# Regrouping the score bursts of the first chunk of each layer in a two-layer attention and MLP kernel

## The chip, the cores and the metric

The kernel runs on one core of one Trainium2 chip, in one launch. The metric is device time in microseconds (us), the median of several runs. Engines are named as the profile names them: PE (TensorE matmul), PEld (its weight loads), ACT (ScalarE), DVE (VectorE), POOL (GpSimd), SP (SyncE, which issues the DMAs).

## What is computed

The reference applies, twice and with the same weights, a sliding-window attention block and an MLP block to 2048 rows of 576 values (bf16):

```
x = x + A(layernorm(x)); x = x + B(layernorm(x))        # and the same once more
A: q,k,v of 32 heads of 18; scores q k^T / sqrt(18), kept where 0 <= i - j < 256;
   softmax; p v; times wo
B: layernorm; gelu(y w1 + b1) with 4608 hidden; times w2; + b2
```

## The kernel before

**Chunks.** The 2048 rows are 16 tiles of 128 rows. Four tiles make a chunk, so that there are four chunks a layer and eight in all, numbered k = 0 to 7. Chunks 0 and 4 are the first of their layers. The stages of a chunk are: layernorm and transposition of its tiles (`ln_norm_T`), projection to q, k, v (`qkv`), scores, softmax numerator and weighted sum for 8 groups of four heads (`E0` for chunk 0, `E` for the others), normalization and output projection with residual and second layernorm (`tail`), MLP up-projection with gelu (`G_part`, in three parts), MLP down-projection (`mm2`). The stages of neighbouring chunks are woven into each other.

**Scores.** A query tile sees its own key tile (masked to a triangle), the one before it in full, and the one two before it (masked to the other triangle). In a chunk that has earlier tiles, that is 12 blocks of 128 by 128 for each head. In the first chunk of a layer there is nothing before the first tile, and 9 blocks are left: key tile 0 with queries 0, 1, 2; key 1 with 1, 2, 3; key 2 with 2, 3; key 3 with 3. `units_of` lists them as bursts of parts `(key tile, first query tile, how many, column)`. `scores` makes one burst: for each part four matmuls, one for each head of the group, in four row strips of the array (32 rows each), into two pairs of PSUM banks; then two exponentials on ACT, one for each pair of heads, from PSUM into a slot of `pT`; then masks on POOL in place. Three pairs of banks exist for this (`SC`), so that the next burst can begin when the first exponential of the one before has been made. There are six slots of `pT` (`PS`). A burst has room for 4 blocks in a bank; before, the first chunks use three bursts a group with three blocks each (384 columns of 512).

**Weighted sum.** `pv` multiplies the masked blocks of a group with v in four column strips, then DVE transposes and normalizes the result.

**Order.** No order is written out. Every step is a `Task` with a cost, a latency, what it reads and writes, and a priority; `Plan.schedule` places the tasks one by one on five engines by these costs, the earliest start first, and the priority among equals. `PL.nudge` is a table of numbers that is added to the priorities of the steps, by stage and part; it does not change what is computed, only the order. Each engine then runs its list strictly in order, with semaphores between them.

**Zero matmuls.** `keep_warm` fills planned gaps of PE longer than 0.4 us in the first 140 us with matmuls of zeros (`warm`), as many as the planned gap divided by `each` gives.

**Array shapes on PE.** Plain matmuls (q, k, v of chunks 0 and 1, down-projection) use the whole array, scores use 32-row strips, `pv` and a narrow form of the down-projection use 32-column strips, and `qkv` from chunk 2 on, `tail` and `G_part` use 64-row strips.

Of the kernel before, what the change touches and what calls it, by code (L numbers as in the profile page):

```python
# [186 lines left out]
class Plan:  # L187
# [61 lines left out]
    def keep_warm(self, a, b, bank_free, extra):  # L249
# [3 lines left out]
        each = 0.2 if a < 8.0 else 0.115  # L253
        n = int((b - a - 0.1) * 0.8 / each)
# [181 lines left out]
def build_kernel(nc, A_x, A_wqkv, A_wo, B_x, B_w1, B_b1, B_w2, B_b2, out):  # L436
# [20 lines left out]
    PVLAG = 1  # L457
# [21 lines left out]
    PL.nudge = {"": -1.63, "b": -20.47, "ea0.0": 108.12, "ea0.1": -112.05, "ea0.p0": -0.32, "ea0.p1": -13.77, "ea0.p2": -108.16,  # L479
# [63 lines left out]

    def sb(name, shape, dtype):
        return nc.alloc_sbuf_tensor(name, shape, dtype)
# [790 lines left out]
```

## Time and profile before

| | |
|---|---|
| device time, median of 3 runs | 857.62 us (857.37 to 857.83) |
| profiled execution: device time / span | 858.81 us / 857.1 us |
| PE busy | 843.6 us (98% of the span), 11968 matmuls |
| ACT busy | 600.2 us (70%), 757 instructions |
| DVE, POOL busy | 399.1 us (47%), 380.0 us (44%) |
| DMA | 119.82 MB, 140 GB/s |

The profiled execution takes 1.19 us longer than the median of the runs. PE is the engine that is almost never idle. A busy PE is not a PE at its peak, since each matmul is counted until its modelled end, beyond the start of the next one. ACT, DVE and POOL have slack over the whole, but not in every stage.

### The profile page before, as it was taken

What the parts mean: (1) busy time and instruction counts of PE and PEld (TensorE: products, weight loads), DVE (VectorE), ACT (ScalarE), POOL (GpSimd) and SP (SyncE); (2) the same over time, 40 slices, a digit from 0 to 9 for tenths busy, and PEclk for the clock granted to TensorE, in tenths of its full rate; (3) what the DMA queues carried; (4) which work ended last, traced back from release to release, by engine and by line L of the source; (5) the groups of instructions that cost most, each with busy time, mean ns of one, the idle gap of its engine ahead of it and who ended that gap; (6) DMA issues with size and microseconds to landing.
All of it is one profiled execution on the core that took longest, in us unless ns stands there. A gap on an engine that the chain in (4) does not pass through costs nothing.

```text
span 857.1 us, 27818 instructions
## 1 busy us (share of the span) xinstructions
PE 843.6 (98%) x11968; PEld 514.4 (60%) x11968; DVE 399.1 (47%) x949; ACT 600.2 (70%) x757; POOL 380.0 (44%) x567
## 2 busy tenths in 40 slices
PE   8999999999999999999999999999999999999998
PEld 6555556656566556665665655666556556556556
DVE  6686425644357442673337723564224534162012
ACT  4988887779657787366773877748777689853730
POOL 4786544476136563154432654426444276322100
PEclk9999999999999999999999999999999999999999
DMA  7899435461496523975457544675435953357320
GB/s 193 197 191 152 119 126 151 115 157 57 153 179 134 182 84 98 186 139 153 114 125 186 97 149 125 121 207 105 133 126 121 276 163 105 121 134 184 117 83 29
DMA packets 181994, 119.82 MB, mean 140 GB/s; under 512 B 107504, under 2 KB 181872, under 8 KB 181872
## 3 DMA queue, kind: packets, MB, share of 16 engines
q1 hardware_dynamic: 181872, 118.05, 55.4%
q8 instruction: 94, 1.54, 0.7%
q14 instruction: 28, 0.23, 0.1%
HBM read 90.10 MB, written 2.36 MB: 108 GB/s over the span
## 4 chain that ended last, share of the span: by engine, by line
PE 92%; DMA 2%; ACT 2%; DVE 2%; issue 1%; POOL 1%; SPq 0%; ACTq 0%; DVEq 0%; POOLq 0%
PE ps L1093 32%; PE ps L777 25%; PE ps L780 10%; PE ps L837 8%; PE ps L909 6%; PE ps L957 5%; PE ps L1048 4%; PE ps L796 1%; ACT pT L919 1%; DMA xnTa<-xn 1%; DMA wqkv<-in_A_wqkv_dram 1%; DMA xnTm<-qn 1%; DVE oq L968 1%; DMA kT<-qn 0%; DVE x_res L1025 0%
## 5 line engine op out<-in xcount | busy, mean ns | idle before, releaser
L940 POOL TENSOR_SCALAR_AFFINE_SELECT pT<-pT 128x512 bf16<-128x512 bf16 (+1 forms) x368 | 283.9, 793 | 224.4 <-ACT pT L919 218.8
L919 ACT ACTIVATE pT<-ps 128x1024 bf16<-128x1024 f32 (+1 forms) x384 | 346.2, 974 | 43.7 <-PE ps L909 42.9
L1093 PE MATMUL ps<-xnTm,w_sb 64*128 64x512 bf16 x2592 | 292.3, 376 | 0.3 <-DVE oq L968 0.2
L1103 ACT ACTIVATE hT<-ps,b1col 128x512 bf16<-128x512 f32 x276 | 167.9, 688 | 173.3 <-PE ps L1093 173.0
L1093 PEld LDWEIGHTS ps<-xnTm,w_sb 64*128 64x128 bf16 x2592 | 126.4, 94 | 141.3 <-issue 4.3
L777 PE MATMUL ps<-w_sb,hT 128*128 128x288 bf16 x1458 | 195.3, 287 | 0.0
L1025 DVE TENSOR_TENSOR x_res<-ps,x_res 128x288 f32<-128x288 f32 x224 | 100.4, 454 | 187.0 <-PE ps L777 127.2
L777 PEld LDWEIGHTS ps<-w_sb,hT 128*128 128x128 bf16 x1458 | 134.8, 98 | 51.3 <-issue 16.1
L837 PE MATMUL ps<-wqkv,xnTa 64*128 64x288 bf16 x1296 | 91.1, 283 | 2.2 <-DMA xnTa<-xn 0.8
L780 PE MATMUL ps<-w_sb,hT 128*32 128x288 bf16 x2616 | 90.3, 286 | 0.2
L861 DVE CAST qn<-ps 128x288 bf16<-128x288 f32 x112 | 46.7, 451 | 80.4 <-PE ps L837 72.6
L968 DVE STREAM_TRANSPOSE oq<-ps 128x512 f32<-128x512 f32 x64 | 45.8, 716 | 80.5 <-PE ps L957 79.5
L837 PEld LDWEIGHTS ps<-wqkv,xnTa 64*128 64x128 bf16 x1296 | 61.3, 94 | 30.0 <-issue 3.8
L780 PEld LDWEIGHTS ps<-w_sb,hT 128*32 128x32 bf16 x2616 | 66.9, 97 | 15.0 <-issue 4.4
L909 PE MATMUL ps<-qT,kT 32*128 32x384 bf16 (+2 forms) x1216 | 64.3, 276 | 2.5 <-ACT pT L919 2.5
L699 POOL TENSOR_SCALAR vtmp<-mv_all 128x1 f32<-128x1 f32 (+2 forms) x45 | 9.2, 204 | 123.4 <-DVE mv_all L690 122.1
L1109 POOL TENSOR_TENSOR x_res<-x_res,b2bc 128x576 f32<-128x576 f32 x32 | 40.2, 1277 | 35.8 <-ACT hT L1103 35.7
L686 DVE BATCH_NORM_STATS2 st_all<-x_res 128x6 f32<-128x288 f32 (+1 forms) x128 | 53.5, 445 | 2.7 <-DMA x_res<-in_A_x_dram 1.9
L849 DVE CAST vA<-ps 128x288 bf16<-128x288 f32 x60 | 25.6, 448 | 60.5 <-PE ps L837 54.6
L957 PE MATMUL ps<-pT,vA 128*20 128x384 bf16 (+2 forms) x1408 | 49.9, 275 | 0.3 <-DVE vA L849 0.2
L909 PEld LDWEIGHTS ps<-qT,kT 32*128 32x128 bf16 x1216 | 19.5, 92 | 42.8 <-issue 29.0
L1048 PE MATMUL ps<-wo_sb,attT 64*128 64x288 bf16 x576 | 43.2, 283 | 0.3
(58 smaller groups left out, 476.8 us busy)
## 6 DMA issues: line engine op xcount, KB each, us to landing
w_sb<-in_B_w_dram SPq DMA_DIRECT2D x46, 864.0 KB, 6.2
w_sb<-in_B_w_dram SPq DMA_DIRECT2D x48, 768.0 KB, 4.7
w_sb<-in_B_w_dram SPq DMA_DIRECT2D x96, 48.0 KB, 4.4
wqkv<-in_A_wqkv_dram SPq DMA_DIRECT2D x3, 576.0 KB, 5.8
x_res<-in_A_x_dram SPq DMA_DIRECT2D x3, 576.0 KB, 4.2
wqkv<-in_B_w_dram SPq DMA_DIRECT2D x2, 864.0 KB, 6.8
out_dram<-x_res SPq DMA_DIRECT2D x12, 144.0 KB, 1.9
xnTm<-xn SPq DMA_TRANSPOSE x36, 2.8
```

What stands on the lines that cost most here:

```text
L777: return e.matmul(bank(b)[:, 0:HB], lhs, rhs, start=start, stop=stop, skip_group_check=True)
L780: ins = e.matmul(bank(b)[32 * j:32 * j + 32, 0:HB], lhs[:, 32 * j:32 * j + 32], rhs, start=start, stop=stop, tile_position=(0, 32 * j), sk ...
L837: ins = e.matmul(bank(bs[o])[:, 0:HB], xnTa[r:r + 64, c, i * 128:(i + 1) * 128], wqkv[r:r + 64, c, col:col + HB], start=(c == 4), stop=(ph ...
L909: ins = e.matmul(two(bs[j // 2])[:, j % 2, col:col + nq * 128], k_of(T0 + so)[0][32 * j:32 * j + 32, g, :], qs[32 * j:32 * j + 32, g, qo * ...
L919: add("act", lambda e, h2=h2: e.activation(pT[:, sl, 2 * h2:2 * h2 + 2, lo:hi], two(bs[h2])[:, :, lo:hi], ACT.Exp, scale=SCALE), reads=[bs ...
L940: add("pool", lambda e, ap=ap, pat=pat, sgn=sgn, kind=kind: e.affine_select(ap, ap, pattern=pat, compare_op=(ALU.is_ge if kind == "d" else ...
L957: ins = e.matmul(bank(bo)[32 * j:32 * j + VW, qo * 128:(qo + nq) * 128], vA[:, (T0 + so) % VS, 8 * j + g, :], pT[:, sl, j, col:col + nq * ...
L968: add("dve", lambda e: e.transpose(oq[:, 0:4 * nt, :].rearrange("p b c -> p (b c)"), bank(bo)[:, 0:nt * 128]), reads=[bo, f"aq{(g - 1) % G ...
L1025: add("dve", lambda e: e.tensor_tensor(x_res[:, t, sl], bank(b)[:, 0:HB], x_old[:, t, sl], ALU.add), reads=[b] + ([f"xin{t}"] if first els ...
L1048: ins = e.matmul(bank(bs[o])[:, 0:HB], attT[r:r + 64, c, i * 128:(i + 1) * 128], wo_sb[r:r + 64, c, col:col + HB], start=(ph == 0 and c == ...
L1093: ins = e.matmul(bank(bks[i])[:, 0:n], w1_sb[r:r + 64, sls[i], col:col + 128], xnTm[r:r + 64, k % 2, c, 0:n], start=(c == 4), stop=(ph == ...
L1103: add("act", lambda e, ff=ff, hd=hd, bk=bk: e.activation(hd[:, 0:n], bank(bk)[:, 0:n], ACT.Gelu_apprx_tanh, bias=b1col[:, ff:ff + 1]), rea ...
```

## The change

There are four edits.

1. In chunks 0 and 4 (`SHARE`) a group has two bursts of four blocks each, which fill the banks: (key 0 with queries 0, 1, 2 and key 1 with query 1), then (key 1 with queries 2, 3 and key 2 with 2, 3). The ninth block, key 3 with query 3, is taken out; `scores9` makes it for four groups at once, in a burst of its own with 4 blocks in a bank and one mask over all of it. `pv` of each group reads its quarter of that slot, and the slot comes free after the fourth group.
2. `keep_warm` reckons 0.215 us for a zero matmul before 8 us, and fills 96% of the planned gap there.
3. The planner's latencies of the first loads (x and the query weights) are raised. The same loads are issued in the same order.
4. The whole table of nudges is replaced, and with it the order of all later steps on all engines.

```
+        each, part = (0.215, 0.96) if a < 8.0 else (0.115, 0.8)
+        n = int((b - a - 0.1) * part / each)
...
-    PL.nudge = {"": -1.63, "b": -20.47, "ea0.0": 108.12, "ea0.1": -112.05, "ea0.p0": -0.32, "ea0.p1": -13.77, "ea0.p2": -108.16,
+    PL.nudge = {"b": 299.87, "ea0.0": 223.17, "ea0.1": 300, "ea0.2": 299.99, "ea0.n0": 300, "ea0.p0": -270.55, "ea0.p1": 39.66,
...
-            cost=0.45 if a < 4 else 0.6, lat=1.4 if a < 4 else 2.0, prio=prio)
+            cost=0.45 if a < 4 else 0.6, prio=prio, **({"lat": 1.2, "move": cnt * 0.64} if a < 4 else {}))
...
+        if k in SHARE:
+            us = [[(0, 0, 3, 0), (1, 1, 1, 384)], [(1, 2, 2, 0), (2, 2, 2, 256)]]
...
+    ninth = {}
+    def scores9(k, g, prio):
+        gs = range(g, g + 4)
+        kept, PL.part = PL.part, f".n{g}"
+        parts = [(3, 3, 1, 128 * n) for n in range(4)]
+        sl = scores(k, g, parts, prio, gs)
+        PL.part = kept
+        for n in gs:
+            ninth[k, n] = ([parts[n - g]], sl)
+    SHARE = (0, 4)
...
     def pv(k, g, units, bo, first, last, prio):
         slots.extend(sl for _, sl in units)
+        if k in SHARE and last:
+            units = units + [ninth[k, g]]
+            if g % 4 == 3:
+                slots.append(ninth[k, g][1])
```

Counted over the whole program, the score bursts go from 192 to 180, the exponentials on ACT from 384 (288 of 1024 elements a partition and 96 of 768) to 360 (all of 1024, the same elements in all), the score matmuls from 1216 to 1280 and those of the weighted sum from 1408 to 1472 (the same columns in more pieces), the zero matmuls from 24 to 36. On PE's list, the places at which the array shape changes from one matmul to the next go from 406 to 388: from 71 to 63 up to the first matmul of `G_part`, from 335 to 325 behind it.

PE's list at the start of the program, before (`warm` are zeros, `ident,xn` are transpositions of a normalized tile, `wqkv,xnTa` the projections of chunk 0, `ident,qn` transpositions of k):

```order
L664 MATMUL ps<-warm 128x256 x8
L673 MATMUL ps<-warm 128x256 x11
L734 MATMUL ps<-ident,xn 128x128 x5
L673 MATMUL ps<-warm 128x256 x3
L796 MATMUL ps<-wqkv,xnTa 128x288 x10
L734 MATMUL ps<-ident,xn 128x128 x4
L796 MATMUL ps<-wqkv,xnTa 128x288 x10
L734 MATMUL ps<-ident,xn 128x128 x6
L796 MATMUL ps<-wqkv,xnTa 128x288 x10
L874 MATMUL ps<-ident,qn 128x128 x8
```

The same place on PE now:

```order
L661 MATMUL ps<-warm 128x256 x8
L670 MATMUL ps<-warm 128x256 x12
L731 MATMUL ps<-ident,xn 128x128 x5
L670 MATMUL ps<-warm 128x256 x6
L731 MATMUL ps<-ident,xn 128x128 x4
L793 MATMUL ps<-wqkv,xnTa 128x288 x5
L731 MATMUL ps<-ident,xn 128x128
L793 MATMUL ps<-wqkv,xnTa 128x288 x5
L731 MATMUL ps<-ident,xn 128x128 x4
L793 MATMUL ps<-wqkv,xnTa 128x288 x20
L871 MATMUL ps<-ident,qn 128x128 x8
L731 MATMUL ps<-ident,xn 128x128 x6
```

One more zero matmul stands ahead of the first transposition and three more behind it; the second tile's transposition comes ahead of the first projection instead of behind its ten matmuls; and between the transpositions of the third and fourth tile and the next projection there is no other matmul.

PE's list around the first score bursts (`qT,kT`), before:

```order
L796 MATMUL ps<-wqkv,xnTa 128x288 x20
L874 MATMUL ps<-ident,qn 128x128 x8
L796 MATMUL ps<-wqkv,xnTa 128x288 x5
L874 MATMUL ps<-ident,qn 128x128 x8
L909 MATMUL ps<-qT,kT 128x384 x4
L796 MATMUL ps<-wqkv,xnTa 128x288 x15
L909 MATMUL ps<-qT,kT 128x384 x4
```

And now (the row `128x128 x16` is the first of the shared bursts):

```order
L793 MATMUL ps<-wqkv,xnTa 128x288 x45
L871 MATMUL ps<-ident,qn 128x128 x8
L793 MATMUL ps<-wqkv,xnTa 128x288 x10
L922 MATMUL ps<-qT,kT 128x384 x4
L922 MATMUL ps<-qT,kT 128x128 x4
L871 MATMUL ps<-ident,qn 128x128 x8
L793 MATMUL ps<-wqkv,xnTa 128x288 x15
L922 MATMUL ps<-qT,kT 128x128 x16
```

From the start of the program, 85 matmuls of projections stand ahead of the first score burst instead of 70, and 36 transpositions instead of 44.

ACT's list around the first exponentials (`pT<-ps`; `kT<-ps` are copies of transposed k, `qn<-ps` of q or k), before:

```order
L878 COPY kT<-ps 128x8x128 x2
L919 ACTIVATE pT<-ps 128x2x384
L858 CAST qn<-ps 128x2x8x18
L919 ACTIVATE pT<-ps 128x2x384 x3
L858 CAST qn<-ps 128x2x8x18
L919 ACTIVATE pT<-ps 128x2x384 x2
L878 COPY kT<-ps 128x8x128
L919 ACTIVATE pT<-ps 128x2x384 x42
```

And now:

```order
L875 COPY kT<-ps 128x8x128
L855 CAST qn<-ps 128x2x8x18
L932 ACTIVATE pT<-ps 128x1024
L875 COPY kT<-ps 128x8x128
L932 ACTIVATE pT<-ps 128x1024
L855 CAST qn<-ps 128x2x8x18
L932 ACTIVATE pT<-ps 128x1024 x2
L875 COPY kT<-ps 128x8x128
L932 ACTIVATE pT<-ps 128x1024 x34
```

Two of the four copies of k now stand behind the first exponential, where one did; of the casts one instead of two. The last row holds 32 exponentials of chunk 0 and two of chunk 1.

More of the change, by code (lines that the diff above doesn't have):

```diff
@@ L631, in xin_load @@
             writes=[f"xin{t}" for t in range(a, a + cnt)], cls="x", ring=4,
-            cost=0.45 if a < 4 else 0.6, lat=1.4 if a < 4 else 2.0, prio=prio)
-    for a, cnt in ((0, 1), (1, 1), (2, 2)):
-        xin_load(a, cnt)
+            cost=0.45 if a < 4 else 0.6, prio=prio, **({"lat": 1.2, "move": cnt * 0.64} if a < 4 else {}))
     def w_load(n, reads=()):
@@ L639, in w_load @@
         dma("sp", wqkv[:, 0:4, n * D:(n + 1) * D], A_wqkv[0:512, n * D:(n + 1) * D].rearrange("(c p) d -> p c d", p=P), reads=reads,
-            writes=[f"w{w}A"], cost=0.5, lat=1.9, prio=-10)
+            writes=[f"w{w}A"], cost=0.5, lat=1.9, prio=-10, **({"move": 2.56} if n == 0 else {}))
         for b in range(2):
@@ L643, in w_load @@
             dma("sp", wqkv[64 * b:64 * b + 64, 4, cols], A_wqkv[512:576, cols], reads=reads, writes=[f"w{w}B{b}"], cost=0.6, prio=-10)
-    w_load(0)
-    w_load(1)
-    w_load(2)
+    for a, cnt in ((0, 1), (1, 1), (2, 2)):
+        xin_load(a, cnt)
+    for n in range(3):
+        w_load(n)
     add("pool", lambda e: e.memset(nhalf[:, :], -0.5), writes=["nhalf"], cost=0.1, prio=-10)
@@ L892, in units_of, with scores @@
             us = [[(0, 0, 3, 0)], [(1, 1, 3, 128)], [(2, 2, 2, 256), (3, 3, 1, 128)]]
+        if k in SHARE:
+            us = [[(0, 0, 3, 0), (1, 1, 1, 384)], [(1, 2, 2, 0), (2, 2, 2, 256)]]
         us = [[p for p in u if t0 + p[0] >= 0] for u in us]
         return [u for u in us if u]
+    ninth = {}
[8 more added lines that the diff above has]
+    SHARE = (0, 4)
     slots = deque(range(PS))
-    def scores(k, g, parts, prio):
+    def scores(k, g, parts, prio, gs=None):
         l, t0, nt = CH[k]
@@ L906, in fn @@
             ins = None
-            for (so, qo, nq, col) in parts:
+            for n, (so, qo, nq, col) in enumerate(parts):
+                gg = gs[n] if gs else g
                 for j in range(4):
-                    ins = e.matmul(two(bs[j // 2])[:, j % 2, col:col + nq * 128], k_of(T0 + so)[0][32 * j:32 * j + 32, g, :],
-                                   qs[32 * j:32 * j + 32, g, qo * 128:(qo + nq) * 128], start=True, stop=True, tile_position=(32 * j, 0),
+                    ins = e.matmul(two(bs[j // 2])[:, j % 2, col:col + nq * 128], k_of(T0 + so)[0][32 * j:32 * j + 32, gg, :],
+                                   qs[32 * j:32 * j + 32, gg, qo * 128:(qo + nq) * 128], start=True, stop=True, tile_position=(32 * j, 0),
                                    skip_group_check=True)
@@ L991, in E0 @@
             lead[g] = [(us[0], scores(0, g, us[0], prio))]
+            if 0 in SHARE and g % 4 == 0:
+                scores9(0, g, prio)
         for g in gs:
@@ L1006, in E @@
                 PL.part = f".{g}"
+                if k in SHARE and n == 0 and g % 4 == 0:
+                    scores9(k, g, prio)
                 units.append((parts, scores(k, g, parts, prio)))
-                while pend and pend[0][0] <= 3 * g + n - PVLAG:
+                while pend and pend[0][0] <= len(us) * g + n - PVLAG:
                     pv(k, *pend.pop(0)[1:], prio - 0.1)
@@ L1011, in E @@
                     done = n == len(us) - 1
-                    pend.append((3 * g + n, g, units, bo, not any(x[1] == g for x in pend) and units[0][0] is us[0], done))
+                    pend.append((len(us) * g + n, g, units, bo, not any(x[1] == g for x in pend) and units[0][0] is us[0], done))
                     units = []
```

2 lines of the change are left out of this document (removed), and 124 rows, old and new, of the table add.

## The prediction

> **What bounds the kernel now.** I read the page first, then PE by stretches of 20 us, then the start and the first chunk's scores row by row.
>
> ```profile
> PE 843.6 (98%) x11968; PEld 514.4 (60%) x11968; DVE 399.1 (47%) x949; ACT 600.2 (70%) x757; POOL 380.0 (44%) x567
> PE 92%; DMA 2%; ACT 2%; DVE 2%; issue 1%; POOL 1%; SPq 0%; ACTq 0%; DVEq 0%; POOLq 0%
> ```
>
> The second row is the chain of work that ended last: PE carries 92% of it. The stretches (PE, PEld, DVE, ACT, POOL busy, then clock, DMA share, GB/s) show where PE is not the bound:
>
> ```profile
> 0.00:20.00 20.00, 16.16 (x127) 12.12 (x128) 13.02 (x41) 8.05 (x17) 8.34 (x26) 0.91 0.74 198
> 20.00:40.00 20.00, 18.70 (x266) 11.37 (x264) 13.26 (x37) 19.11 (x28) 13.76 (x23) 1.00 0.85 202
> 40.00:60.00 20.00, 18.45 (x292) 10.59 (x292) 17.10 (x39) 19.53 (x27) 17.91 (x28) 1.00 0.97 169
> 60.00:80.00 20.00, 19.21 (x314) 11.28 (x310) 15.58 (x41) 15.44 (x23) 12.87 (x26) 1.00 1.04 185
> 80.00:100.00 20.00, 19.10 (x270) 10.09 (x274) 8.54 (x23) 16.80 (x26) 13.01 (x18) 1.00 0.57 121
> ...
> 580.00:600.00 20.00, 19.15 (x291) 11.71 (x290) 9.28 (x20) 16.48 (x17) 14.21 (x20) 1.00 0.38 100
> ...
> 720.00:740.00 20.00, 19.48 (x272) 10.78 (x264) 5.54 (x10) 17.27 (x23) 9.21 (x12) 1.00 0.43 136
> ...
> 840.00:860.00 20.00, 14.26 (x117) 11.15 (x114) 4.63 (x11) 0.00 (x0) 0.00 (x0) 0.97 0.06 23
> ```
>
> PE idles 13.5 us of the span. 8.4 of them lie in the first 100 us, 2.8 at the very end (14.26 busy of 17.1), and 2.2 between, where no stretch has more than 0.85. From 20 to 60 us ACT is full (19.1 and 19.5 of 20): there the exponentials of chunk 0 set the pace and PE waits for them. So whatever the change saves on PE counts in full behind the first up-projection (86 us); ahead of it, the start and ACT decide.
>
> **The change part by part.** *Shape changes on PE.* Two rows of one down-projection with a score burst between them, from PE's timeline, and two lengths of the same matmuls from the chain:
>
> ```profile
> 103.01 1.65 PE L777 MATMUL ps<-w_sb,hT 128*128 128x288 bf16 x12
> 104.59 0.40 PE L909 MATMUL ps<-x_res,kT 32*128 32x256 bf16 x8
> 104.92 1.64 PE L777 MATMUL ps<-w_sb,hT 128*128 128x288 bf16 x12
> ```
> ```profile
> 161.31 3.05 PE ps L777 x24
> 164.69 1.58 PE ps L777 x12
> ```
>
> Twelve more matmuls take 3.05 - 1.58 = 1.47 us, 0.1225 each. From 103.01 to 104.92 are 1.91 us; less 1.47 leaves 0.44 for the burst. Its 512 columns, four heads side by side, stream in 0.22 at the same rate. The other 0.22 are its two shape changes, 0.11 each. Behind the first up-projection the list has 10 changes fewer: -1.1 us, on the path. The 8 that go ahead of it are worth 0.9, but in a stretch that ACT sets; I count them at nothing.
>
> *More and smaller pieces.* 64 score matmuls and 64 of the weighted sum are added, at equal columns.
>
> ```profile
> 102.68 0.34 PE L909 MATMUL ps<-x_res,xnTm 32*128 32x384 bf16 x4
> 102.85 0.22 PE L909 MATMUL ps<-x_res,kT 32*128 32x128 bf16 x4
> ```
>
> Four matmuls of 128 columns take 103.01 - 102.85 = 0.16, and 0.05 without the shape change: they run side by side at the streaming rate, so that smaller pieces cost nothing. One page of the Trainium skill speaks against this edit: TensorEngine Tiling (Array Packing), Instruction Overhead, gives each matmul some 60 cycles of overhead and warns against small pieces; 128 matmuls by 25 ns would be an estimated 3.2 us, and the sum +2.1 instead of -1.1. The rows show no such overhead at 128 columns; what no row has is four sets of 128 in one burst.
>
> *The clock at the start.* The first projection waits for the query weights; then its ten matmuls run at half clock (PE busy, clock, DMA, GB/s in three windows of 3.41 us):
>
> ```profile
> 0.99:4.41 3.42, 3.37 (x16) 1.00 0.69 182
> 4.41:7.82 3.41, 1.34 (x13) 1.00 1.03 343
> 7.82:11.23 3.41, 2.68 (x14) 0.50 0.98 301
> ```
> ```profile
> 3.30 5.11 DMA wqkv<-in_A_wqkv_dram
> 8.55 2.56 PE ps L796 x10
> 11.45 1.23 PE ps L796 x10
> 14.30 0.45 PE ps L874 x8
> ```
>
> A window with 1.34 us of matmuls was followed by one at half clock, one with 2.68 by full clock. The loss is 2.56 - 1.23 = 1.3 us. Now one more zero matmul ahead of the first transposition, three more behind it (256 columns each, 0.11 by the streaming rate), and the second tile's four transpositions fall into the middle window, about 0.7 us more, some 2.0 in all. That lies between 1.34 and 2.68, so I give half a chance that the clock stays. By the Trainium skill (TensorE: Matmul & The Clock Gate, What's actually happening) the clock drops only after an idle window; by that it would stay for certain. The trace disagrees: the window ahead of the drop held 13 matmuls.
>
> *The first score burst.* These are the rows of PE (with the first up-projection) and ACT there:
>
> ```profile
> 20.75 0.34 PE L909 MATMUL ps<-qT,kT 32*128 32x384 bf16 x4
> ...
> 86.14 11.83 PE L1093 MATMUL ps<-xnTm,w_sb 64*128 64x512 bf16 x108
> ```
> ```profile
> 13.65 0.71 ACT L737 COPY xnTa<-ps 128x640 bf16<-128x640 bf16 x1
> 14.79 1.01 ACT L878 COPY kT<-ps 128x1024 bf16<-128x1024 bf16 x1 [0.28 <-PE ps L874]
> 21.77 0.82 ACT L919 ACTIVATE pT<-ps 128x768 bf16<-128x768 f32 x1
> 26.53 1.08 ACT L878 COPY kT<-ps 128x1024 bf16<-128x1024 bf16 x1
> 27.43 4.55 ACT L919 ACTIVATE pT<-ps 128x768 bf16<-128x768 f32 x6
> 48.91 12.26 ACT L919 ACTIVATE pT<-ps 128x768 bf16<-128x768 f32 x16 [0.15 <-PE ps L909]
> 75.33 1.01 ACT L919 ACTIVATE pT<-ps 128x1024 bf16<-128x1024 f32 x1
> 77.29 1.94 ACT L919 ACTIVATE pT<-ps 128x1024 bf16<-128x1024 f32 x2
> ```
>
> From 8.55 PE now has 85 projections at 0.1225 and 27 transpositions at 0.056 (0.45 for 8) to the first burst: 10.4 + 1.5, so 20.5. New waits come on top: the third tile's projection now stands right behind the transpositions, with only the ACT copy (0.71) and two hand-overs between them, 0.8; the fourth tile's copy then comes behind a copy of k (1.01 + 0.71 against 1.23 us of projections), 0.5; and 0.3 for the key weights and the last copy of k. First burst at 22.1 instead of 20.75, first exponential at 22.6 instead of 21.77 (it no longer stands behind three copies of k). With the half clock: 23.6.
>
> *Exponentials of chunk 0.* Before, they last from 21.77 to 59.2 (48.91 + 12.26, less the two of chunk 1 in that row, 1.94): 37.5 us, with one copy of k (27.43 - 26.53 = 0.9) and two casts (0.3 each), so that 36.0 remain for 48, 0.75 each with 1.0 us of gaps. Now 36 of 1024 elements at 1.94 - 1.01 = 0.93 make 33.5, with the same gaps 34.5: -1.5. The bounds: nothing, if time went by elements alone; -2.7 by the means of the forms below (48 by 0.824 against 36 by 1.024). Two copies of k and one cast fall among them: +0.9 - 0.3 = +0.6. So chunk 0's exponentials end at 22.6 + 34.5 + 2.1 = 59.2 with full clock, where they end now, and at 60.2 with half clock. Behind that point PE has the same work left as before. The start and ACT together: 0 (to +1.0; and -1.2 from the lower bound of the exponentials).
>
> ```profile
> L919 ACT ACTIVATE pT<-ps 128x1024 bf16<-128x1024 f32 x288 | 274.8, 1024 | 28.8 <-PE ps L909 28.6
> L940 POOL TENSOR_SCALAR_AFFINE_SELECT pT<-pT 128x512 bf16<-128x512 bf16 x256 | 163.6, 653 | 194.1 <-ACT pT L919 192.7
> L940 POOL TENSOR_SCALAR_AFFINE_SELECT pT<-pT 128x1024 bf16<-128x1024 bf16 x112 | 124.5, 1111 | 30.3 <-ACT pT L919 26.1 <-PE ps L777 2.0 <-PE ps L909 1.1
> L919 ACT ACTIVATE pT<-ps 128x768 bf16<-128x768 f32 x96 | 71.5, 824 | 14.9 <-PE ps L909 14.3
> ```
>
> *Masks.* A group had 4 masks of 512 and one of 1024: 3.72 us. Now 5 of 512 and a quarter of one of 2048, which no row shows; by 0.458 for each further 512 elements it takes 2.0: 3.77. POOL stays under ACT (4.5 exponentials by 0.93, 4.2 a group). But the first weighted sum now waits for the shared mask and all of the group's, about 0.9 us of ACT idle, in place of the 1.0 of gaps already counted. *Later shared bursts, slots of pT, order of DMAs*: one slot of six is held for four groups, which leaves 5 for two bursts a group instead of 6 for three; the fourth q transposition is issued ahead of the tiles' transpositions on SP, which land long before chunk 1's projections need them. Nothing for both. *Eight new zero matmuls at 58 to 86 us* go where PE is planned idle; 60 to 100 us has 1.7 us of idle to cover their 0.9. I take 0; uncovered they cost 0.9.
>
> The sum is -1.1: span 857.1 to 856.0, own time 858.81 to 857.7, and in the runs' median, which lies 1.19 below the profiled execution, 857.62 to 856.5.
>
> **The rivals.** *B, the new order takes more:* the same loads are planned later and closer to what they take, and if the list fits the real times better, the single waits behind 100 us shrink too (0.85 at 580, 0.52 at 720, 2.2 in all), and the gain on ACT comes as -2.7 instead of -1.5: -1.1 - 1.2 - 1.1 (half of the later idle) = -3.4, 854.2. For it: ACT was full where chunk 0 was late. Against it: the waits behind 100 us are already few, and a new order can make others. *C, the start is late and stays late:* half clock (+1.0), zero matmuls uncovered (+0.9), and the new list puts one or two new waits of the size of the worst now (0.85) behind the first up-projection, +1.1 on average: -1.1 + 3.0 = +1.9, 859.5. It decides from a first exponential later than 23.6 us. For it: 15 more projections stand ahead of the first burst, the two new waits, and PE stands in front of the first weighted sum until POOL is done. Against it: PE has all of chunk 1's projections to fill in. *D, small pieces do not run side by side* where four sets of 128 follow each other, as the page's rule would have it: each of the 32 added sets takes 4 by 0.056 instead of 0.05, 0.17 more, 5.4 us: 861.9. The rows of 128 columns speak against it.
>
> **How the numbers follow.** A measurement of this kernel can tell 0.2% from no change, 1.7 us. The forecast A has 0.50, with its own range from 855.3 (exponentials at their bound) to 857.5 (half clock): 0.12 of it is faster by over 1.7 us, 0.38 within. B has 0.30, all faster. C has 0.17 and D 0.03, both slower. So faster 0.42, same 0.38, slower 0.20. The range reaches into B beyond its middle and to C's middle, 853.4 to 859.4, and leaves out D, the far half of C and the far end of B.
>
> **What would show it.** The ten first projections in 1.23 us, or 2.56 again; the first exponential at 22.6 us; chunk 0's exponentials in 36.6 us with 0.93 each; the first up-projection at 86.1, give or take 1; behind it, PE's time from there to the end shorter by 1.1; the four sets of 128 in a shared burst in 0.2 to 0.3 us. The prediction is wrong if the first up-projection moves by over 2 us, or if the part behind it changes by other than 0.5 to 1.7.

## The result and the profile after

The changed kernel takes 862.55 us (860.42 to 863.76, six runs), the kernel before on the same chip 857.73 us (857.32 to 858.76, six runs): ratio 1.0052, 95% interval 1.0038 to 1.0065. It is slower by about 4.5 us (3.3 to 5.6 by the interval), and lies 3.15 us above the range. Its profiled execution took 861.57 us, with a span of 859.8. That is below its median, while the profiled execution of the kernel before lies above its own, so that the two profiles, which the following readings rest on, differ by 2.7 us only.

The page's row of engines and its chain of waits, of the changed kernel:

```profile
PE 844.9 (98%) x12360; PEld 523.3 (61%) x12360; DVE 396.9 (46%) x949; ACT 597.6 (70%) x733; POOL 380.9 (44%) x571
PE 89%; DMA 4%; DVE 2%; ACT 2%; POOL 1%; issue 1%; SPq 1%; POOLq 0%; DVEq 0%
```

PE's share of the chain fell from 92% to 89%, and DMA's rose from 2% to 4%. The first five stretches of 20 us (PE, PEld, DVE, ACT, POOL busy, then clock, DMA share, GB/s):

```profile
0.00:20.00 20.00, 18.02 (x142) 13.34 (x143) 14.49 (x45) 8.40 (x17) 9.06 (x27) 1.00 0.90 212
20.00:40.00 20.00, 17.23 (x198) 10.30 (x200) 11.27 (x32) 16.53 (x20) 13.50 (x22) 0.85 0.65 177
40.00:60.00 20.00, 19.32 (x398) 11.62 (x390) 17.02 (x38) 19.04 (x21) 16.04 (x25) 0.98 0.90 163
60.00:80.00 20.00, 18.53 (x311) 10.75 (x310) 16.31 (x43) 16.58 (x23) 14.60 (x27) 1.00 0.83 182
80.00:100.00 20.00, 17.65 (x218) 10.01 (x218) 8.82 (x24) 14.90 (x23) 12.30 (x20) 1.00 0.55 115
```

The start is better than before: the clock is 1.00 over the first 20 us, where it was 0.91. From 20 to 40 us PE and ACT both lose (ACT 16.53 instead of 19.11), and the clock is 0.85. Of the 844.9 us of PE, some are matmuls at half clock.

The part behind the first up-projection, once for the kernel before and once for the changed kernel, and the row with which it begins there:

```profile
86.14:857.10 770.96, 765.89 (x10888) 465.65 (x10884) 337.33 (x788) 532.20 (x656) 322.83 (x460) 1.00 0.53 135
```
```profile
89.88:859.80 769.92, 764.25 (x11200) 472.57 (x11200) 332.35 (x784) 527.28 (x642) 320.19 (x458) 1.00 0.54 135
```
```profile
89.88 2.33 PE L1114 MATMUL ps<-xnTm,w_sb 64*128 64x512 bf16 x20 [1.62 <-DMA xnTm<-xn]
```

So that part is shorter by 1.04 us, as forecast (1.1). The whole loss, 89.88 - 86.14 = 3.74 us, comes ahead of it, in a stretch that was forecast at nothing. The sizes of single profiles scatter: in the profiles of the experiments below this part takes 769.7 to 771.3 us with the kernel before's grouping (e3, e4, e16) and 768.6 to 770.0 with the changed one (e1, e2, e5, e6, e9, e10, e12 to e15).

**Where PE stands.** PE's timeline of the changed kernel around the first weighted sum (start, duration, and in brackets the wait ahead and what ended it), two rows of the kernel before, and three windows of the changed kernel's clock:

```profile
30.36 1.40 PE L774 MATMUL ps<-wqkv,xnTm 128*128 128x288 bf16 x10
31.80 0.40 PE L922 MATMUL ps<-qT,kT 32*128 32x256 bf16 x8
34.68 0.21 PE L1210 MATMUL ps<-ident,hT 36*128 36x36 bf16 x1 [2.48 <-DMA hT<-in_B_b_dram]
34.82 1.14 PE L974 MATMUL ps<-pT,vA 128*20 128x384 bf16 x20
...
36.44 2.58 PE L774 MATMUL ps<-wqkv,xnTm 128*128 128x288 bf16 x10
```
```profile
31.80 0.67 PE L957 MATMUL ps<-pT,vA 128*20 128x384 bf16 x16
...
35.54 0.19 PE L1189 MATMUL ps<-ident,hT 36*128 36x36 bf16 x1
```
```profile
30.61:34.02 3.41, 1.54 (x18) 0.81 (x15) 2.25 (x8) 3.41 (x5) 3.32 (x6) 1.00 0.78 253
34.02:37.43 3.41, 2.75 (x34) 1.41 (x35) 2.75 (x10) 1.35 (x2) 2.98 (x6) 0.50 0.27 55
37.43:40.85 3.42, 3.42 (x43) 1.78 (x45) 1.44 (x4) 2.30 (x4) 1.23 (x2) 0.50 0.52 99
```

PE stands idle from 32.2 to 34.7 us ahead of the transposition of the up-projection's bias (b1, the row `ident,hT`), which the new order places right in front of the first weighted sum. The bias itself is not later: by the completion counts in the trace it lands at 34.63 us, and at 35.20 in the kernel before. But there PE comes to it at 35.54 us, behind the first weighted sum and 15 projections, and does not wait. The clock of the changed kernel is then halved for two windows, 6.8 us: ten projections take 2.58 us instead of 1.40. Later PE stands 0.89 us ahead of 60.94 (first scores of chunk 1), 0.33 ahead of 77.75, and 1.62 ahead of the first up-projection.

The bias is not the only thing that PE would wait for here. The first weighted sum needs POOL's masks, and eight of them run in a row until 33.95 us:

```profile
29.06 4.89 POOL L953 TENSOR_SCALAR_AFFINE_SELECT pT<-pT 128x512 bf16<-128x512 bf16 x8 [0.74 <-ACT pT L932]
```

The projections next on PE's list wait for VectorE. Its timeline, first of the changed kernel, then of the kernel before:

```profile
30.14 0.46 DVE L858 CAST qn<-ps 128x288 bf16<-128x288 f32 x1 [0.16 <-PE ps L774]
31.77 1.18 DVE L683 BATCH_NORM_STATS2 st_all<-x_res 128x6 f32<-128x288 bf16 x3 [1.18 <-DMA x_res<-in_A_x_dram]
...
34.56 0.41 DVE L683 BATCH_NORM_STATS2 st_all<-x_res 128x6 f32<-128x288 bf16 x1
34.88 0.44 DVE L858 CAST qn<-ps 128x288 bf16<-128x288 f32 x1
```
```profile
31.80 0.46 DVE L861 CAST qn<-ps 128x288 bf16<-128x288 f32 x1 [0.15 <-PE ps L780]
32.18 0.45 DVE L686 BATCH_NORM_STATS2 st_all<-x_res 128x6 f32<-128x288 bf16 x1
32.55 0.70 DVE L968 STREAM_TRANSPOSE oq<-ps 128x512 f32<-128x512 f32 x1
33.17 0.42 DVE L686 BATCH_NORM_STATS2 st_all<-x_res 128x6 f32<-128x288 bf16 x1
33.51 0.23 DVE L971 RECIPROCAL rinv<-oq 128x16 f32<-128x16 f32 x1
33.66 0.39 DVE L861 CAST qn<-ps 128x288 bf16<-128x288 f32 x1
```

Before, the statistics of chunk 2's rows (`st_all`) stand almost all singly between other steps. Now eight of them follow one another with only their own aggregations between them, wait 1.18 us for the rows, and end at 35 us. Two casts of chunk 1's projections stand behind them, and hold the two PSUM banks that PE's next projections need (e1 below shows PE's wait for them).

The third place is SyncE's queue, of the changed kernel, with PE's row that waits for it:

```profile
39.63 5.52 SPq L623 DMA_DIRECT2D wo_sb<-in_A_wo_dram  x9
46.01 2.43 SPq L623 DMA_DIRECT2D w_sb<-in_B_w_dram  x3
48.48 1.52 SPq L623 DMA_DIRECT2D wo_sb<-in_A_wo_dram  x3
50.05 1.24 SPq L877 DMA_TRANSPOSE x_res<-qn  x1
...
57.33 1.32 SPq L877 DMA_TRANSPOSE x_res<-qn  x1
```
```profile
60.94 0.34 PE L922 MATMUL ps<-x_res,xnTm 32*128 32x384 bf16 x4 [0.89 <-ACT pT L932]
```

The twelve loads of the output projection's weights read the first group's attention output as a starting signal, which now comes at 38.7 us instead of 34.4. They and a load of w1 hold the queue to 50 us, and the transpositions of chunk 1's queries and keys, with some of chunk 2's tiles, follow one after another until 61. By the completion counts in the trace the one issued at 57.33 landed at 60.73, 0.2 us ahead of the burst; the exponential that the row names had ended at 60.24.

### The profile page after: what moved, and what is told of

Same layout as the page of the kernel before. It is cut to its first block, busy times and chain, and to the rows that moved or that the text cites. A ratio compares the mean times of both kernels' runs of the same rounds, so it can differ in the third digit from the quotient of the medians.

```text
span 859.8 us, 28551 instructions
## 1 busy us (share of the span) xinstructions
PE 844.9 (98%) x12360; PEld 523.3 (61%) x12360; DVE 396.9 (46%) x949; ACT 597.6 (70%) x733; POOL 380.9 (44%) x571
## 4 chain that ended last, share of the span: by engine, by line
PE 89%; DMA 4%; DVE 2%; ACT 2%; POOL 1%; issue 1%; SPq 1%; POOLq 0%; DVEq 0%
PE ps L1114 31%; PE ps L774 23%; PE ps L777 11%; PE ps L834 9%; PE ps L922 6%; PE ps L974 5%; PE ps L1069 3%; DMA xnTm<-xn 3%; ACT pT L932 1%; PE ps L793 1%; DMA hT<-in_B_b_dram 1%; SPq L623 1%; DVE xn L714 0%; POOL rstd L698 0%; POOL pT L953 0%
## 5 line engine op out<-in xcount | busy, mean ns | idle before, releaser
L932 ACT ACTIVATE pT<-ps 128x1024 bf16<-128x1024 f32 x360 | 343.0, 1029 | 41.9 <-PE ps L922 41.5
L1114 PEld LDWEIGHTS ps<-xnTm,w_sb 64*128 64x128 bf16 x2592 | 130.9, 94 | 139.9 <-issue 5.4
L774 PE MATMUL ps<-w_sb,hT 128*128 128x288 bf16 x1374 | 184.3, 287 | 1.5 <-DVE x_res L1046 1.1
L774 PEld LDWEIGHTS ps<-w_sb,hT 128*128 128x128 bf16 x1374 | 126.9, 98 | 50.5 <-issue 17.8
L777 PE MATMUL ps<-w_sb,hT 128*32 128x288 bf16 x2952 | 100.0, 286 | 0.2
L777 PEld LDWEIGHTS ps<-w_sb,hT 128*32 128x32 bf16 x2952 | 76.6, 97 | 15.0 <-issue 3.6
L922 PE MATMUL ps<-qT,kT 32*128 32x128 bf16 (+2 forms) x1280 | 62.4, 271 | 0.9 <-ACT pT L932 0.6
L974 PE MATMUL ps<-pT,vA 128*20 128x256 bf16 (+2 forms) x1472 | 51.4, 274 | 0.2 <-POOL xn L722 0.2
L714 DVE TENSOR_SCALAR xn<-x_res,mv_all,rstd 128x576 bf16<-128x576 f32 (+1 forms) x60 | 34.0, 572 | 19.9 <-POOL rstd L698 11.0
```

Of the source, the lines that this page charges most:

```text
L774: return e.matmul(bank(b)[:, 0:HB], lhs, rhs, start=start, stop=stop, skip_group_check=True)
L777: ins = e.matmul(bank(b)[32 * j:32 * j + 32, 0:HB], lhs[:, 32 * j:32 * j + 32], rhs, start=start, stop=stop, tile_position=(0, 32 * j), sk ...
L922: ins = e.matmul(two(bs[j // 2])[:, j % 2, col:col + nq * 128], k_of(T0 + so)[0][32 * j:32 * j + 32, gg, :], qs[32 * j:32 * j + 32, gg, qo ...
L932: add("act", lambda e, h2=h2: e.activation(pT[:, sl, 2 * h2:2 * h2 + 2, lo:hi], two(bs[h2])[:, :, lo:hi], ACT.Exp, scale=SCALE), reads=[bs ...
L974: ins = e.matmul(bank(bo)[32 * j:32 * j + VW, qo * 128:(qo + nq) * 128], vA[:, (T0 + so) % VS, 8 * j + g, :], pT[:, sl, j, col:col + nq * ...
L1114: ins = e.matmul(bank(bks[i])[:, 0:n], w1_sb[r:r + 64, sls[i], col:col + 128], xnTm[r:r + 64, k % 2, c, 0:n], start=(c == 4), stop=(ph == ...
```

## The experiments

Each run is timed beside the kernel before on its chip; ratios are to that, with a 95% interval. e1, e2, e5, e6, e9, e10 and e12 to e15 start from the changed kernel, e3, e4, e11 and e16 from the kernel before, e7 and e8 from a mixture. Unless shown otherwise, an edit moves steps in the list that `Plan.schedule` has made (`order`), so that nothing else changes.

**The bias loaded first, and the stand filled with zeros.**

```
e1: +  b1 = order.pop(position of the load of b1)
    +  order.insert(position of the first load of w1, b1)
e2: +  24 zero matmuls ahead of the transposition of b1
```

> The changed kernel, with one thing moved: the load of the bias b1 is issued on SP ahead of the first load of MLP weights instead of behind the second; all other lists are as they were. Theory 1 (the late bias): PE stood 2.6 us at the transposition of b1, because its load was queued behind two weight loads, and the window with that wait brought half clock from 34.0 to 40.9 us. Without it both go, and the first up-projection comes 3.5 to 5 us earlier than at 89.9: about 858. Theory 2 (the masks): the weighted sum of group 0, next on the list, would have waited for POOL's masks until 34.0 anyway. Then the wait only shrinks by 0.8 us, the clock still halves, and the time stays at 861 to 862.

> The changed kernel, with 24 zero matmuls (2.6 us at full clock) ahead of the transposition of b1, so that PE is busy while it waits, and nothing moved. If the half clock behind the wait is a loss of its own, its 6.8 us at half rate go and with them 2 to 3 us: 859.5 to 860.5. If ACT sets the pace there, the half clock was hidden, and the time stays at 862.5. If the wait is not there in an execution, the zeros cost up to 2.6 us: 863 to 865.

Measured: e1 1.0055 [1.0036, 1.0073], e2 1.0055 [1.0042, 1.0069]. Neither gains. PE's timeline of e1:

```profile
32.27 0.40 PE L925 MATMUL ps<-qT,kT 32*128 32x256 bf16 x8
34.19 0.17 PE L1213 MATMUL ps<-ident,hT 36*128 36x36 bf16 x1 [1.52 <-ACT pT L935]
...
36.65 0.66 PE L777 MATMUL ps<-wqkv,xnTm 128*128 128x288 bf16 x2 [1.18 <-DVE qn L861]
```

With the bias there, the transposition waits for an exponential to free its bank, and the projection behind it for VectorE's cast. The bias was only the last of several. The masks are another, as the second theory had it: in e1 POOL's eight masks end at 34.42 us and the first weighted sum starts at 34.47. In e2 the clock stayed whole at 34 us, and the loss moved: the first scores of chunk 1 waited 2.88 us until 61.58, and a half clock from 60.8 to 67.6 followed.

**The kernel before, with a late bias or a better start.**

```
e3: the second load of w1 issued ahead of b1, in the kernel before
e4: -        n = int((b - a - 0.1) * 0.8 / each)
    +        n = 20 if 4.0 < a < 8.0 else int((b - a - 0.1) * 0.8 / each)
```

> The kernel before, with the second load of MLP weights issued ahead of the load of b1, as the changed kernel has it. The bias then lands 2.5 to 3.5 us later than at 35.2 us, where PE comes to its transposition at 35.5. Theory 1 (a late bias alone costs this much, whatever the grouping): PE waits 2 to 3 us, the clock halves behind it, 860 to 863. Theory 2 (it is the masks and the grouping): PE has slack to ACT here, the wait is absorbed, 857.5 to 858.5.

> The kernel before, with 20 zero matmuls instead of 3 behind the first transposition, so that PE is busy until the query weights land and the clock does not halve behind that wait. As predicted for the start: the ten first projections in 1.2 instead of 2.6 us, the first score burst 1.3 us earlier, and at most that much of the whole: 856.4 to 857.4. If the start is bound by loads and transpositions, nothing: 857.7.

Measured: e3 1.0035 [1.0022, 1.0047]; e4 0.9985 [0.9973, 0.9997]. PE's timeline of e3:

```profile
37.18 0.19 PE L1193 MATMUL ps<-ident,hT 36*128 36x36 bf16 x1 [1.84 <-DMA hT<-in_B_b_dram]
37.30 0.67 PE L961 MATMUL ps<-pT,vA 128*20 128x384 bf16 x16
37.90 0.34 PE L913 MATMUL ps<-qT,kT 32*128 32x384 bf16 x4
38.17 1.38 PE L781 MATMUL ps<-wqkv,xnTm 128*128 128x288 bf16 x5
```

A stand of 1.84 us at this place costs the kernel before some 3 us, with nothing regrouped: the five projections behind it run at half clock (1.38), and its first up-projection moves to 89.60 (another wait in this execution, 1.34 us ahead of 68.02, is part of that). So the place is as dear as the changed kernel suggests. In e4's profile the first score burst comes 1.06 us earlier and the first up-projection 0.42 later (86.56): PE waits 1.00 us ahead of 64.03 and 0.17 ahead of 64.99 for two transpositions that stand behind a load of w2. In this execution, 858.70 us, the earlier start is eaten ahead of 86 us; over eleven runs (median 858.06) it is worth 0.15%.

**The queue.**

```
e5: the 12 loads of wo without reads=["aq0"], ahead of chunk 1's first transposition;
    the third load of w1 behind four more transpositions
e6: e5 with the zeros of e2
```

> The changed kernel with one edit of the SyncE queue: the twelve loads of the output projection's weights no longer wait for the first group's attention output and are issued at about 30 us, where the queue stands idle for 5 us, and the third load of up-projection weights is issued behind four more transpositions. In the changed kernel those fifteen loads hold the queue from 39.6 to 50.0 us while the queries and keys of chunk 1 that were cast from 43 us on wait behind them. Theory 1 (the late first weighted sum costs through this queue): the transpositions go out from about 45 us, the first score burst of chunk 1 no longer waits 0.96 us, the up-projection starts 1 to 1.5 us earlier than in the changed kernel (89.9 us), and the time is about 861, ratio to the kernel before 1.0035. The wait of 2.5 us at 32 to 34.7 us and the half clock behind it stay. Rival (the queue is no limit, the exponentials are): no change, ratio 1.0052, and the wait at 59 to 61 us stays.

> The edit of the queue and 24 zero matmuls ahead of the transposition of b1, which fill the wait at 32 to 34.7 us. The zero matmuls alone moved the loss: the clock stayed whole at 34 us, but the first score burst of chunk 1 then waited 2.96 us at 58 to 61.6 us and the clock halved there (ratio 1.0055). Theory 1: with the transpositions out earlier that wait shrinks to under 1 us, no half clock follows, and the up-projection starts at about 87 us, 2.5 to 3 us earlier than in the changed kernel; time about 858.8, ratio 1.001. Rival (exponentials): the wait at 58 us stays over 2 us with the half clock behind it, ratio about 1.005.

Measured: e5 1.0069 [1.0056, 1.0081] and e6 1.0092 [1.0078, 1.0105]. e6 is worse than the changed kernel, and e5's interval overlaps with that kernel's. My edit was badly made: the weight loads from 29.4 us on follow right behind b1, which landed later (PE stood 3.48 us until 35.17; that they are the reason is not shown), and the load of w1 now stood at 55.0, ahead of the very transposition that the burst waits for (issued 56.86, landed 61.71). The rival does not follow either, since the wait moved with that landing.

**Second layer alone.** The kernel before with `SHARE = (4,)` and the new table's numbers for chunks 4 to 7.

> The kernel before with the regrouping in the second layer's first chunk alone (chunk 4) and the changed table's entries for chunks 4 to 7; the start, the first chunk and the order of everything up to the second layer are those of the kernel before. Behind the first up-projection it has 12 fewer changes of array shape than the kernel before (the changed kernel has 10 fewer). If each is worth 0.1 us on the path, the first up-projection stands at 86.1 us as before and the time is 1.1 to 1.3 us lower: 856.6, ratio 0.9986. Rival (what the part behind gained in the changed kernel came from its later start, not from the regrouping): no difference, ratio 1.0000.

> The same with 20 zero matmuls instead of 3 behind the first transpositions, which keep the clock whole at the start (alone they gave a ratio of 0.9985 [0.9973, 0.9997]). If the two gains add up: 855.3 to 856, ratio 0.9972. If the start's gain is given back by 65 us, as the profile of it alone showed (first up-projection at 86.6 us), it is that of the run before: 0.9986.

Measured: e7 1.0629 [1.0608, 1.0650] and e8 1.0636 [1.0621, 1.0650], 53 to 55 us slower, with waits of 4.2 to 6.9 us on PE at about 400, 515 and 736 us and half clock behind them. Half of one table and half of the other make an order that fits neither, so that this says nothing on the regrouping: that the 1.04 us behind the first up-projection come from the shape changes stays argued, not shown. The new order of that part is a rival that no run takes out.

**The order of chunk 1's tiles.** The changed kernel transposes the queries of tiles 0, 3, 1, 2 in this order (the kernel before 2, 1, 0, 3); the first burst reads 0, 1 and 2.

```
e9:  queue: qx1, kx1, qx2, xa0, qx3, k5, k4      (was qx3, k5, xa0, qx1, kx1, qx2, k4)
e10: e9 with the zeros of e2
e11: kernel before, qx0 and kx0 behind qx3
```

> The changed kernel with six transpositions of the SyncE queue in another order. Its table transposes the queries of chunk 1 in the order tile 0, 3, 1, 2, and the kernel before in the order 2, 1, 0, 3; the first score burst of chunk 1 reads the queries of tiles 0, 1 and 2. Here the order is 0, 1, 2, 3. In the changed kernel the transposition of tile 2's queries is issued at 57.33 us, lands at 60.73, and the burst starts at 60.94. Theory 1 (the order of the queue makes the burst wait): issue at about 53, landing by 57, no wait of 0.96 us ahead of the burst; the up-projection starts about 1 us earlier, time about 861.5, ratio 1.004; the wait at 32 to 34.7 us and the half clock behind it stay. Rival (exponentials set the pace here): nothing changes, 1.0052.

> The same order of the queue and 24 zero matmuls ahead of the transposition of b1. The zero matmuls alone kept the clock whole at 34 us and then lost 2.96 us in the wait for the first score burst of chunk 1 and 2.13 us in a half clock behind it, since tile 2's queries landed at 61.38. Theory 1: those queries land by 57, that wait and the half clock go, the first up-projection stands at 86 to 87.5 us, and the time is about 858.7: ratio 1.000 to 1.001. Rival: the burst goes on waiting over 2 us, now for something else, and the ratio stays at about 1.005.

> The kernel before with the opposite edit: the transpositions of tile 0's queries and keys of chunk 1, which its first score burst reads, are issued behind those of tile 3's queries instead of ahead of them. Theory 1: they land at about 60 to 61 us instead of by 57.3, the burst waits about 2 us at 58.7, with or without a half clock behind it, and the time is 2 to 4 us longer: ratio 1.002 to 1.005. Rival: no difference, 1.000.

Measured: e9 1.0046 [1.0029, 1.0062], e10 1.0048 [1.0033, 1.0064]. As forecast, the first scores of chunk 1 waited no longer (they start at 58.91 in e9 and nothing halves there); but the time hardly moved. PE and SyncE's queue in e9:

```profile
74.00 2.00 PE L1074 MATMUL ps<-wo_sb,attT 64*128 64x288 bf16 x26
79.23 1.38 PE L839 MATMUL ps<-wqkv,xnTa 64*128 64x288 bf16 x10 [3.23 <-DMA xnTa<-xn]
```
```profile
71.66 0.66 SPq L628 DMA_DIRECT2D w_sb<-in_B_w_dram  x1
72.42 1.22 SPq L742 DMA_TRANSPOSE xnTa<-xn  x1
```

The next wait, 0.33 us in the changed kernel, grew to 3.23: PE came to it 1.4 us earlier, and chunk 2's last tile, which stands behind a load of w2 of 864 KB, landed at 79.19, 6.8 us after its issue. In the changed kernel it stands behind the same load and landed 5.4 us after its issue, so that the load is not the whole of it. e11 (1.0113) is no test: the moved transpositions read buffers that the next tile's casts have overwritten, and its stand of 7 us is on another cast.

**Work into the first stand.** All earlier cures had failed, so these two put useful work there and then mended the queue as well.

```
e12: e1, and
     DVE: three casts of chunk 1's projections ahead of chunk 2's statistics
     PE:  ten matmuls of chunk 1's projections ahead of the transposition of b1
e13: e12 and e9, and the second load of w2 behind chunk 2's last transposition
```

> The changed kernel with useful work in its first long wait. On VectorE the casts of chunk 1's first projections (tile 0) stand ahead of the statistics of chunk 2's rows, which wait for a load until 33 us, instead of behind them; on TensorE two projections of chunk 1 (ten matmuls) that followed the first weighted sum stand ahead of the transposition of b1, and b1 is loaded first. Theory (that wait is the cause): TensorE stands under 0.7 us between 32 and 35 us instead of 2.6, the clock stays whole there, the first up-projection comes 1.5 to 3 us earlier than 89.9, and the time is 859 to 861: ratio 1.001 to 1.003. Rival (each wait that goes is replaced by the next, because the exponentials and transpositions that follow set the pace): first up-projection still behind 89 us, ratio 1.005.

> The same with the queries of chunk 1 transposed in the order tile 0, 1, 2, 3, and the second load of down-projection weights issued behind the transposition of chunk 2's last normalized tile instead of ahead of it (in the run with the queue's order alone, that tile was issued at 72.4 us behind this load, landed at 79.2, and TensorE waited 4.2 us for it, with a half clock behind it). Theory: no wait over 1 us between 30 and 86 us, the clock whole from 6 us on, the first up-projection at 86 us or earlier; with the 1.1 us that the part behind it gained: 856.5 to 858, ratio 0.998 to 0.9995, no worse than the kernel before. Rival: ratio 1.003 or more, with a new wait over 1.5 us in the profile.

Measured: e12 1.0023 [1.0010, 1.0035], e13 1.0011 [1.0000, 1.0022]. PE's timeline of e12:

```profile
32.61 1.40 PE L793 MATMUL ps<-wqkv,xnTm 128*128 128x288 bf16 x10
34.20 0.17 PE L1229 MATMUL ps<-ident,hT 36*128 36x36 bf16 x1 [0.19 <-ACT pT L951]
34.48 0.67 PE L993 MATMUL ps<-pT,vA 128*20 128x384 bf16 x20
35.09 0.40 PE L941 MATMUL ps<-qT,kT 32*128 32x256 bf16 x8
38.04 0.40 PE L941 MATMUL ps<-qT,kT 32*128 32x384 bf16 x8 [2.56 <-DVE b1col L1231]
```

The stand ahead of b1 is gone, and with it more than half of the loss (0.52% to 0.23%); with the queue's orders four fifths of it (0.11%), with the first up-projection at 87.70. The step from e12 to e13 lies within their intervals. What is left in both is one stand of 2.56 us at 35 to 38 us, for the bank that the cast of b1 frees, behind the same statistics, and a half clock for one window behind it (39.2 to 42.6 us in e13). e13 keeps the regrouping, so the order of the steps between 30 and 80 us, not the regrouping itself, accounts for most of the loss; that was the theory. (What the same moves would give the kernel before was not tried.) What stays in every such version is the later first weighted sum: in e13 POOL's masks end at 34.10 us and it starts at 34.16, where the kernel before starts it at 31.80. The forecast of e13 was still too good by 0.2%, since the stand at 35 us remained.

**The statistics later still.**

```
e14: e13, chunk 2's statistics in two halves behind the first group's weighted sum
e15: the same without the queue's two edits
```

> The run with all orders mended, and on VectorE the statistics of chunk 2's rows (3.2 us) behind the first group's weighted sum and the cast of b1 instead of ahead of them, in two halves, with the two steps on GpSimd that follow each. Theory (VectorE's order is the cause): the wait of 2.75 us at 35 to 38 us falls under 0.7, the clock is whole from 6 us on, the first up-projection comes at 85 to 86 us, and the time is 856 to 857.5: ratio 0.997 to 0.9988, below the kernel before. Rival (exponentials and masks set the pace ahead of the second weighted sum, whatever VectorE does): the wait stays over 1.5 us, ratio 1.001.

> The same without the two edits of the SyncE queue (tile order of chunk 1's transpositions, second load of down-projection weights). Theory: no wait between 30 and 40 us; the waits at 59 and 74 us that hang on the queue stay or grow, since TensorE comes to them earlier, and the first up-projection comes 1.5 to 2.5 us later than in the run with both: ratio 0.9995 to 1.0015. Rival (the queue's orders are only an echo of the first wait): the same time as the run with both.

Measured: e14 1.0033 [1.0022, 1.0044], e15 1.0036 [1.0023, 1.0049]. My theory fell here, and e15 came out as its rival had it: the same time without the queue's two edits as with them. So no pair of runs shows a gain from the queue. PE's timeline of e14:

```profile
36.69 0.40 PE L958 MATMUL ps<-qT,kT 32*128 32x384 bf16 x8 [1.13 <-ACT pT L968]
...
38.92 1.39 PE L813 MATMUL ps<-wqkv,xnTm 128*32 128x288 bf16 x20 [1.23 <-DVE qn L894]
...
47.16 0.67 PE L1010 MATMUL ps<-pT,vA 128*20 128x384 bf16 x20 [0.91 <-POOL pT L989]
```

One stand became three, for exponentials, a cast and a mask, and the half clock stayed for one window (38.8 to 42.3 us). The kernel before spreads the eight statistics almost one by one; two halves are not that. Whether such a spread would bring the last 0.11% back was not tried, nor was the kernel before's place of b1 on PE's list.

**A version below both.** The kernel before with the zeros of e4 and its first load of w2 behind the two transpositions that PE waited for in e4.

> The kernel before with 20 zero matmuls instead of 3 at the start (alone: ratio 0.9985 [0.9973, 0.9997]) and its first load of down-projection weights issued behind the transpositions of chunk 2's second tile and chunk 1's last keys instead of ahead of them. With the zeros alone these were issued at 57.3 and 60.1 us behind that load (55.2 us, landed at 60.9) and landed at 64.0 and 64.9, and TensorE stood 1.66 us between 61.5 and 65 us. If the load in front of them is what makes them late: they land 2 to 3 us earlier, that wait falls to under 0.5 us, the first up-projection stands at 85.3 us instead of 86.6, and the time is about 856.5: ratio 0.997 to 0.9975. Rival (they wait for VectorE or for each other, not for the load): 0.9985 again.

Measured: 857.15 us (856.21 to 858.58, eleven runs), the kernel before 858.44 (857.52 to 861.05, fifteen runs): 0.9984 [0.9975, 0.9993], 0.16% faster than the kernel before and so faster than both. In its profile the wait is gone (the transpositions landed at 59.67 and 61.55 instead of 64.0 and 64.9, the first up-projection starts at 84.79, and the execution took 856.22). But the ratio is that of e4: that the queue's edit adds to the zeros is seen in one profile and not in the medians.

## Why the prediction was wrong

*Right in size, with the cause open: the part behind the first up-projection*, 1.04 us shorter against 1.1. Two profiles of one grouping can differ by as much: e16, which has the kernel before's grouping and PE's list of that part, takes 769.7 us there against 771.0. *Right: the exponentials and the mask.*

```profile
21.25 1.03 ACT L932 ACTIVATE pT<-ps 128x1024 bf16<-128x1024 f32 x1 [0.29 <-PE ps L922]
36.55 1.94 ACT L932 ACTIVATE pT<-ps 128x1024 bf16<-128x1024 f32 x2 [2.06 <-PE ps L922]
53.72 7.44 ACT L932 ACTIVATE pT<-ps 128x1024 bf16<-128x1024 f32 x8 [0.26 <-PE ps L922]
```

Eight take 7.44 us, 0.93 each. The shared mask took 2.01 us. *Right: small pieces.* The shared burst starts at 23.63 and the projection behind it at 23.96, 0.33 us with its two shape changes: as long as any other burst of 512 columns, so that rival D is out.

*Right in sign, too small: the start.* I put the middle window at some 2.0 us of matmuls and gave the clock half a chance; it stayed. In this execution the clock's windows, counted back from 34.02 in steps of 3.41, begin at 3.29 and 6.71 us and hold 3.22 and 2.79 us. In e1, e5, e13, e14 and e15, which start the same way, a window begins at 4.2 to 5.1 us and holds 1.87 to 2.21, near the 2.0, and the clock stayed there too. (By the Trainium skill, TensorE: Matmul & The Clock Gate, What's actually happening, it drops only behind an idle window. The start agrees; at 34.02 us the trace disagrees again, as the window ahead of that drop held 18 matmuls, 1.54 us.) The first burst came at 20.81 instead of 22.1, the first exponential at 21.25 instead of 22.6, as the new waits that I added up were not there. Being early did not reach the first up-projection.

*Wrong: the step that set the start and ACT together at 0 (to +1.0).* That stretch cost 3.74 us. The step took ACT as its bound and let PE follow. Chunk 0's exponentials ended at 53.72 + 7.44 = 61.16 instead of 59.2, although they began 1.35 us early: 39.9 us for 36, of which 33.5 are exponentials, 2.1 two copies of k and a cast, and 4.3 gaps. The first gap, 2.06 us, is at the first weighted sum, where I had written 0.9 in place of another 1.0. I had asked what ACT waits for there, not what PE waits for. Nor did PE have "the same work left as before" in the same time behind that point: from the end of these exponentials to the first up-projection are 28.7 us instead of 26.9, with two of the waits above (0.33 and 1.62). So of the 3.74 us some 1.9 are lost by the end of the exponentials and 1.8 behind it. My argument against rival C, that PE has chunk 1's projections to fill in, is what failed: they were on the list, but behind the transposition of b1, and their banks were held by casts that stood on VectorE behind statistics. e12, which moves both, starts the ten projections at 32.61 us and takes away more than half of the loss. I had not read VectorE's order at all, nor the new place of b1 on PE's list.

*Wrong: "order of DMAs ... Nothing for both".* I had followed one transposition. The new table also turned the order of chunk 1's tiles so that the last query transposed is one that the first burst needs, and the loads of wo start from a signal that comes 4 us later. PE stood 0.89 us for that burst. What this cost in the end stays open: e9 took that wait away and gained nothing.

*The rivals.* C had the right sign and the nearest number (859.5, 3 us too low), but not its mechanism: it should decide from a first exponential later than 23.6 us, and that came at 21.25. It did name the place, as an argument for it ("PE stands in front of the first weighted sum until POOL is done"), but its price counted waits behind the first up-projection instead, and no rival had the half clock behind such a stand.

## What to carry to other kernels

A change that replaces the whole order of a list is judged by the order of every engine that can hold a bank or a queue, not by the engine that is full: read what stands ahead of each cast, and what stands ahead of each transposition in the DMA queue. Where several waits hang on each other, taking away one may show nothing (six runs here, two of them badly made, stayed at 1.0046 or above); put work into the first one before the later ones are judged. Numbers tuned for one grouping and mixed with those for another lost 53 us in the one mixture that was tried.

## What the hardware did that I had not expected

The clock halves in whole windows of 3.41 us, mostly one or two of them, behind a window with little work on PE: 1.54 us of matmuls were followed by two at half clock (34.02 to 40.85), though PE was busy 2.75 us in the first of these; and a stand of 3.2 us in e9 by two more. Over all traces of this case, without their first and last microseconds, the border is narrow: the 26 windows that a half clock followed hold up to 1.74 us of matmuls, and all that a whole clock followed hold 1.79 or more, but for one of 1.63 in e6. So a stand of 2 to 3 us costs up to 3.4 us again behind it (an estimate: 6.8 us at half clock), and where it falls in a window decides: a stand of 2.78 us in e9 was followed by one window at half clock, that of 2.48 us in the changed kernel by two. The runs of the changed kernel spread over 3.3 us, those of the kernel before over 1.4 beside them and over 4.7 beside e1 to e4, and e10, whose profiled execution had a whole clock throughout (859.44 us), over 5.2. A transposition right behind a load of 864 KB landed 5.4 us (changed kernel) and 6.8 us (e9) after its issue; in e13, where that load is issued behind it, it took 2.7.
